# Moving two swaps and a broadcast one step later, and one transpose ahead, in a fused attention kernel

## The chip, the cores and the metric

The kernel runs on one core of a Trainium2 chip. A core has five engines that run their own instruction streams side by side: TensorE (PE; its weight loads are shown as PEld), VectorE (DVE), ScalarE (ACT), GpSimd (POOL) and SyncE (SP), which here does nothing but issue DMAs. DMAs issued by SP and by POOL are carried by the same 16 DMA engines. The metric is the device time of one execution in microseconds (us), the median over runs.

## The reference

Three layers follow one another, all in fp32. Attention with pooled queries comes first; its output is cut into tokens for a dense layer with the Mish activation, and that layer's output goes to eight experts whose gates come from a Sinkhorn iteration.

```python
q_pool = q.reshape(B, H, S // 2, 2, D).mean(axis=3)          # B=2, H=8, S=1152, D=64
scores = scale * np.matmul(q_pool, k.transpose(0, 1, 3, 2))
scores = scores - np.max(scores, axis=-1, keepdims=True)
attn = np.exp(scores)
attn = attn / (np.sum(attn, axis=-1, keepdims=True) + 1e-09)
x = np.matmul(attn, v)                                        # -> tokens (1152, 512)
h = x @ w_in;  x = (h * np.tanh(softplus(h))) @ w_out         # w_in (512, 2048)
P = sinkhorn(exp(x @ w_gate))                                 # 8 rounds, 8 experts
out = sum(P[:, e:e+1] * (np.maximum(x @ w1[e], 0) @ w2[e]) for e in range(8))
```

The change touches the attention alone.

## The kernel before

Every fp32 product is made of parts: a value is split into a rounded high part and a low rest (names ending in h and l), and the high and low parts are multiplied separately into one sum. For the attention, one 128-column weight tile carries high and low of 64 head dimensions side by side, and the second copy with the halves swapped gives the cross products.

The attention works on 8 pairs of heads. A pair has 2 x 576 pooled queries, that is 9 tiles of 128 queries (t = 0 to 8; t = 4, the middle one, belongs half to each head). One loop runs over all 72 tiles; its body, one step (number g, pair p, tile t), works on several tiles at once:

- PE makes the scores of tile g (psS, line 478), DVE evacuates them and takes the row minimum of the negated scores (e, line 483), ACT takes the exponential with its row sum (line 497).
- In step g + 1 SP issues the hand-over of that tile, a DMA from `e` to `er` (line 503) that copies the tile as it is into another buffer. `er` has two buffers: the hand-over of tile g can start only when PE has transposed tile g - 2.
- In step g + 3 PE transposes tile g out of `er` (psT, line 560), ACT and DVE evacuate it in halves (eth, line 563; etl, line 566), and over the steps after that PE multiplies it with V (psA, line 581).

Beside these run the preparations of the next pair, a little in each step. POOL splits K, V and Q and issues their loads (kraw, vraw, qraw). PE transposes the split K in thirds (psk, line 410) and the split Q in three pieces (psq, line 456): the first, u = 0, in step t = 6 of the pair before, the second, u = 1, in step t = 1, the third, u = 2 (the middle tile), in step t = 0. ACT copies each piece out (qT, line 463; qz, line 429). A piece then needs a second copy with its two 64-row halves exchanged: `swap` (line 450), two SBUF-to-SBUF DMAs. The first piece is used from t = 0 of its pair, the middle one at t = 4, the second from t = 5.

The row sums of a pair are finished after its last tile: `turn_sums` (line 510) runs at the end of step t = 1 of the next pair. PE turns the sums, DVE copies them (rt, line 515), SP writes them to DRAM (row, line 520) and reads them back broadcast over the partitions in three DMAs (rx, line 526). POOL multiplies the pair's output with rx at the end of step t = 5 (xs, line 607).

What sets the order: all of it is written out by hand, each engine runs its instructions in program order, and SP is one queue. An SP instruction that waits holds everything behind it. Work for SP that has to wait for a result is put in the list `first` and issued at the start of the next step, ahead of that step's hand-over:

```python
waiting = first + loads
first[:], loads[:] = [], []
for f in waiting:
    f()
...
if pre:
    pre.pop(0)()            # the first transposes of this step, ahead of psT
...
    transposes(g - LAG)     # psT, LAG = 3
if g <= NQ:
    hand_over(g - 1)        # e -> er
```

The other transposes of a step (what is left in `pre`) come after its psA, ahead of its exponential.

Of the kernel before, what the change touches and what calls it, by code (L numbers as in the profile page):

```python
# [23 lines left out]
def pool_attention_mish_sinkhorn_kernel(  # L24
# [22 lines left out]
    NPAIR = B * H // 2  # L47
# [59 lines left out]
    def run(t, eng, most=99):  # L107

        q = queue[eng]
        while q and q[0][0] <= t and most > 0:  # L110
            q.pop(0)[1]()
            most -= 1
# [185 lines left out]
    with ExitStack() as actx:  # L298
        def pool(name, bufs, **kw):
            return actx.enter_context(tc.tile_pool(name=name, bufs=bufs, **kw))  # L300
# [29 lines left out]
        for i in range(2):  # L330
            t = z_p.tile([P, 2, 2, P], F32R, name=f"qz{i}")
# [2 lines left out]

        raws, kst, vst, kT, qst, qT = {}, {}, {}, {}, {}, {}
        loader = nc.sync
        loads, first = [], []

        def heads(p):
            b, hp = divmod(p, HPB)  # L340
# [78 lines left out]
        def q_tile(p, x):  # L419
            u, i = divmod(x, MID)  # L420
            if (p, u) not in qT:
                qT[p, u] = qt_p.tile([P, 2, MID, P], F32R, tag="qT", name=f"qT{p}_{u}", bufs=2)
            return qT[p, u], i

        def middle(p, ps, n):

            z = qz[p % 2]
            for j in range(2):
                nc.scalar.activation(
                    z[:, 0:n, j, j * D:(j + 1) * D], ps[:, 0:n, j * D:(j + 1) * D].bitcast(F32), AF.Copy)  # L430
# [16 lines left out]
        def swap(t):  # L447

            for a, b in ((0, D), (D, 0)):
                nc.sync.dma_start(out=t[a:a + D, 1].bitcast(F32), in_=t[b:b + D, 0].bitcast(F32))  # L450

        def trans_q(p, u):
            ps = ps_t.tile([P, 4, P], F32R, tag="t", name=f"psq{p}_{u}")
            n = min(MID, QTL - MID * u)
            for i in range(n):
                nc.tensor.transpose(  # L456
                    ps[:, i, :], qst[p][:, MID * u + i, 0:2, :].rearrange("p a d -> p (a d)"), identr)
            if u == 2:
                middle(p, ps, 1)
                t = qz[p % 2]  # L460
            else:
                t, _ = q_tile(p, MID * u)
                nc.scalar.activation(t[:, 0], ps[:, 0:n].bitcast(F32), AF.Copy)
            first.append(lambda: swap(t))

        scS, eS, erS, rsS, rxS = {}, {}, {}, {}, {}

# [42 lines left out]
        def turn_sums(p):  # L510

            ps = ps_t.tile([P, 4, P], F32, tag="t", name=f"psr{p}")
            nc.tensor.transpose(ps[0:QTL, 0, :], rsS.pop(p), ident)
            rt = rx_p.tile([QTL, P], F32, tag="rt", name=f"rt{p}")
            nc.vector.tensor_copy(rt, ps[0:QTL, 0, :])
            row = row_p.tile([QTL, P], F32, tag="row", name=f"row{p}")
            rx = rxS[p] = rx_p.tile([P, SQ], F32, tag="rx", name=f"rx{p}")

            def out():
                nc.sync.dma_start(out=row, in_=rt)  # L520
                first.append(back)

            def back():
                flat = row.rearrange("t p -> (t p)")
                for j, x, a, n in ((0, 0, 0, SQ), (1, 0, SQ + D, SQ - D), (1, SQ - D, SQ, D)):
                    nc.sync.dma_start(
                        out=rx[j * D:(j + 1) * D, x:x + n], in_=flat[a:a + n].unsqueeze(0).to_broadcast([D, n]))

            first.append(out)
# [86 lines left out]
        def run_av(n):  # L616
            for _ in range(n):
                if av_todo:
                    av_todo.pop(0)()
# [79 lines left out]
        def turn(p, t):  # L699
            fs = []  # L700
            for j in range(2):
                pp = p + (j == 0)
                if pp < NPAIR:
                    fs += [
                        lambda pp=pp, j=j, c=c: trans_k(pp, j, c)
                        for c in range(3) if TURN["k10" if p == 0 and j == 1 else f"k{j}"][c] == t]
            for u in range(3):
                pp = p + (u == 0)
                if p == 0 and TURN["q0"][u] == t:
                    fs.append(lambda u=u: trans_q0(u + 2))  # L710
                if 0 < pp < NPAIR and TURN["q"][u] == t:
                    fs.append(lambda pp=pp, u=u: trans_q(pp, u))
            return fs

        for g in range(T0 + EARLY):
            p, t = divmod(g, QTL)
            if g == 1:
                bctx.close()
                ps_t = pool("ps_t", 4, space=PSUM)
                ps_a = pool("ps_a", 1, space=PSUM)  # L720
            pre = turn(p, t) if g < NQ else []
            waiting = first + loads
            first[:], loads[:] = [], []
            for f in waiting:
                f()
            if g < LAG:
                exps(g)
                for f in pre:
                    f()
                if g + 1 < LAG:  # L730
                    split_kv(0, 0, "v", nc.gpsimd, g)
                    scores(g + 2, ps_s)
            else:
                if LAG < g < NQ:
                    scores(g)
                if p and g < NQ:
                    prep(p, t)
                if g < T0:
                    run(g, "dve")
                if pre:  # L740
                    pre.pop(0)()
                if t == 7 and 0 < p < NPAIR:
                    run_av(4)
                ready = len(av_todo)
                if g < NQ + LAG:
                    transposes(g - LAG)
                if g <= NQ:
                    hand_over(g - 1)
                if not p:
                    prep(p, t)  # L750
                run_av(min(ready, (5 if t == 6 and 0 < p else 9) if g < NQ else 18))
                for f in pre:
                    f()
                if g < NQ:
                    exps(g)
            if p and t == 0:
                row_sums(p - 1)
            if p and t == 1:
                turn_sums(p - 1)
            if late:  # L760
                late.pop(0)()
            if g < T0:
                run_all(g)
            if g == QTL:
                load_gate()
            if g == NQ - 1:
                sctx.close()
                ps_o = ctx.enter_context(tc.tile_pool(name="ps_o", bufs=3, space=PSUM, side="right"))
                wpools["d0"] = ctx.enter_context(tc.tile_pool(name="wd0", bufs=1, side="right"))
                mctx = ExitStack()  # L770
                wpools["d1"] = mctx.enter_context(tc.tile_pool(name="wd1", bufs=1, side="right"))
                wpools["t"] = mctx.enter_context(tc.tile_pool(name="wt2", bufs=3, side="right"))
            if g >= T0:
                mish_step(g - T0)
# [559 lines left out]
```

## Time and profile before

| What | Value |
|---|---|
| Median of 3 runs | 1222.17 us (1221.45 to 1222.9) |
| The profiled execution | 1223.26 us |
| Its span, first to last instruction | 1221.5 us, granted TensorE clock 1.000 |
| PE busy | 1203.7 us, 99% of the span |
| DVE, POOL, ACT busy | 855.8, 654.0, 592.1 us |
| Chain that ended last | PE 90%, DVE 5%, DMA 4%, ACT 1%, issue 1% |
| Largest DMA group | er<-e, 70 issues of 576.0 KB, 4.1 us to landing (median) |

The chain says on what the end of the program hung, step by step backwards; the engine with the largest share of it is the one whose work or waiting set the time. The attention occupies about the first 262 us, 72 steps of some 3.5 us each; behind it come the dense layer and the experts. In the rows below, a DMA issue is shown on `SPq` with the line that issued it, `x3` says that three were merged into one row, and a bracket such as `[0.93 <-DMA er<-e]` gives the idle time of the engine just before the instruction and what ended it.

### The profile page before, as it was taken

The page shows a single profiled execution, that of the slowest core. Times are in us where ns is not written, and L with a number is a line of the kernel's source. Part 1 is how long each engine was busy: PE and PEld are TensorE (multiplying, and loading weights), DVE is VectorE, ACT ScalarE, POOL GpSimd, SP SyncE. Part 2 cuts the span into 40 slices and gives each one's busy share as a digit, 9 for nine tenths or more (in the row PEclk, how much of TensorE's full clock was granted, in tenths as well). Part 3 has the DMA queues.
Part 4 walks back from the last instruction along what each step waited for, and adds up shares of the span by engine and source line. Part 5 has one row for each costly group of instructions (what it writes and reads, how often), then busy time and mean ns, then how long its engine had stood idle before and what let it go on. Part 6 is the DMA issues. An engine that isn't in the chain of part 4 may idle for free.

```text
span 1221.5 us, 19362 instructions
## 1 busy us (share of the span) xinstructions
PE 1203.7 (99%) x6840; PEld 1110.4 (91%) x6840; DVE 855.8 (70%) x1598; ACT 592.1 (48%) x1354; POOL 654.0 (54%) x752
## 2 busy tenths in 40 slices
PE   8899999999999999999999999999999999999998
PEld 8899999999999999898888889999888889999887
DVE  7899999876444333787866677766866777866865
ACT  7888889877544443543332233333333233333331
POOL 7667777415444331485755566555555565555551
PEclk9999999999999999999999999999999999999999
DMA  6787787653223210011111111111011111111112
GB/s 202 265 281 263 272 264 255 232 179 120 88 71 98 74 31 30 1 52 53 32 38 45 52 48 49 52 52 52 23 40 52 53 44 52 53 52 38 37 39 78
DMA packets 51985, 116.39 MB, mean 95 GB/s; under 512 B 7977, under 2 KB 22897, under 8 KB 51889
## 3 DMA queue, kind: packets, MB, share of 16 engines
q1 hardware_dynamic: 48400, 103.36, 25.9%
q0 software_dynamic: 3488, 11.80, 3.3%
q8 instruction: 54, 0.88, 0.3%
q14 instruction: 43, 0.34, 0.1%
HBM read 66.86 MB, written 2.40 MB: 57 GB/s over the span
## 4 chain that ended last, share of the span: by engine, by line
PE 90%; DVE 5%; DMA 4%; ACT 1%; issue 1%; POOL 0%; POOLq 0%; ACTq 0%
PE po L1237 30%; PE c L1067 26%; PE ph L231 10%; PE po L806 8%; PE psS L478 4%; PE psA L581 4%; DMA er<-e 4%; PE psT L560 3%; DVE e L483 2%; DVE etl L566 1%; PE psk L410 1%; PE psw L646 0%; ACT eth L563 0%; PE pg L861 0%; PE psq L456 0%
## 5 line engine op out<-in xcount | busy, mean ns | idle before, releaser
L83 POOL TENSOR_TENSOR wslotsl<-s,wslotsh 128x256 fp32r<-128x256 f32 x180 | 132.0, 743 | 237.1 <-ACT wslotsh L76 237.1
L1245 DVE SCALAR_TENSOR_TENSOR oacc<-po,Pm,oacc 128x512 f32<-128x512 f32 (+1 forms) x217 | 161.1, 746 | 102.2 <-PE po L1237 95.8
L1237 PE MATMUL po<-wdbl,hhall 128*128 128x512 f32 (+1 forms) x543 | 214.4, 395 | 0.0
L1237 PE MATMUL po<-wdbh,hlall 128*128 128x512 f32 (+1 forms) x543 | 214.1, 394 | 0.0
L1237 PE MATMUL po<-wdbh,hhall 128*128 128x512 f32 (+1 forms) x543 | 214.0, 394 | 0.0
L1084 ACT ACTIVATE t<-c 128x384 f32<-128x384 f32 x80 | 39.3, 491 | 246.2 <-PE c L1067 246.2
L1104 ACT ACTIVATE hhall<-c 128x384 fp32r<-128x384 f32 x180 | 88.6, 492 | 127.4 <-DVE c L1100 124.7
L1237 PEld LDWEIGHTS po<-wdbh,hhall 128*128 128x128 f32 x543 | 102.1, 188 | 24.3
L1237 PEld LDWEIGHTS po<-wdbl,hhall 128*128 128x128 f32 x543 | 102.1, 188 | 23.3
L1237 PEld LDWEIGHTS po<-wdbh,hlall 128*128 128x128 f32 x543 | 102.1, 188 | 23.2
L83 POOL TENSOR_TENSOR wslotsl<-rawu,wslotsh 128x256 fp32r<-128x256 f32 x120 | 90.9, 772 | 49.8 <-ACT wslotsh L76 49.8
L483 DVE TENSOR_SCALAR_CACHE_REDUCE e<-psS 128x1152 f32<-128x1152 f32 x72 | 97.3, 1352 | 22.0 <-PE psS L478 11.7
L566 DVE TENSOR_TENSOR etl<-psT,eth 128x384 fp32r<-128x384 f32 (+1 forms) x240 | 108.0, 507 | 4.8 <-ACT eth L563 4.2
L563 ACT ACTIVATE eth<-psT 128x384 fp32r<-128x384 f32 (+1 forms) x240 | 92.8, 477 | 15.6 <-PE psT L560 15.2
L1105 DVE SCALAR_TENSOR_TENSOR hlall<-c,hhall 128x384 fp32r<-128x384 f32 x180 | 98.7, 548 | 2.1
L1067 PE MATMUL c<-x2l,wslotsh 128*128 128x384 f32 x280 | 94.3, 337 | 0.0
L1067 PE MATMUL c<-x2h,wslotsl 128*128 128x384 f32 x280 | 94.1, 336 | 0.0
L1067 PE MATMUL c<-x2h,wslotsh 128*128 128x384 f32 x280 | 93.8, 335 | 0.0
L497 ACT ACTIVATE e<-e,nm 128x1152 f32<-128x1152 f32 x70 | 89.3, 1276 | 0.1
L175 POOL TENSOR_TENSOR wt<-wt,raw 128x512 int32<-128x512 int32 x32 | 42.4, 1325 | 84.0 <-DVE wt L169 59.8
L478 PE MATMUL psS<-kT,qT 128*128 128x384 f32 x384 | 81.9, 348 | 2.8 <-DVE e L483 2.7
L76 ACT ACTIVATE wslotsh<-s 128x256 fp32r<-128x256 f32 x180 | 72.0, 411 | 24.3 <-DVE s L1033 24.3
(365 smaller groups left out, 3117.2 us busy)
## 6 DMA issues: line engine op xcount, KB each, us to landing
er<-e SPq DMA_DIRECT2D x70, 576.0 KB, 4.1
rawd<-in_moe_w_dram SPq DMA_DIRECT2D x60, 256.0 KB, 2.7
rawu<-in_moe_w_dram SPq DMA_DIRECT2D x30, 384.0 KB, 3.3
raw<-in_moe_w_in_dram SPq DMA_DIRECT2D x16, 512.0 KB, 4.3
raw<-in_moe_w_out_dram SPq DMA_DIRECT2D x16, 512.0 KB, 3.7
vraw<-in_v_dram POOLq DMA_DIRECT2D x15, 288.0 KB, 4.7
kraw<-in_k_dram POOLq DMA_DIRECT2D x13, 288.0 KB, 4.6
qT<-qT SPq DMA_DIRECT2D x28, 128.0 KB, 3.1
```

The costliest lines, as they stand in the source:

```text
L83: eng.tensor_tensor(out=lo, in0=src, in1=hi.bitcast(F32), op=ALU.subtract)
L231: nc.tensor.matmul(ps[:, 0:TH], lhsT=a, rhs=b, start=(n == 0), stop=(n == len(ops) - 1))
L478: nc.tensor.matmul(ps[:, kb, 0:TH], lhsT=a, rhs=kt[:, kb * TH:(kb + 1) * TH], start=(n == 0), stop=(n == len(ops) - 1))
L483: nc.vector.tensor_scalar(sc, ps[:, :, 0:TH], -1.0, None, op0=ALU.mult, op1=ALU.min, accum_out=nm)
L497: nc.scalar.activation(e, sc, AF.Exp, bias=nm, scale=-1.0, accum_out=rsS[p][:, t:t + 1])
L563: nc.scalar.activation(eh[:, cs, o:o + b - a], ps[:, 0:3, a:b], AF.Copy)
L566: nc.vector.tensor_tensor(out=el[:, cs, o:o + b - a], in0=ps[:, 0:3, a:b], in1=eh[:, cs, o:o + b - a].bitcast(F32), op=ALU.subtract)
L806: nc.tensor.matmul(ps[:, 0:TH], lhsT=a, rhs=b, start=(n == 0), stop=(n == len(ops) - 1))
L1067: nc.tensor.matmul(cb[c], lhsT=a_, rhs=b_, start=FIRST[n] and m == 0, stop=LAST[n] and m == len(ops) - 1, skip_group_check=True)
L1105: los.append(lambda: nc.vector.scalar_tensor_tensor(out=lo, in0=b, scalar=0.0, in1=hi.bitcast(F32), op0=ALU.max, op1=ALU.subtract))
L1237: nc.tensor.matmul(ps[:, 0:w], lhsT=a, rhs=b[:, cs], start=(n == 0), stop=(n == len(ops) - 1))
L1245: nc.vector.scalar_tensor_tensor(out=oa, in0=ps[:, 0:w], scalar=gate, in1=oa, op0=ALU.mult, op1=ALU.add)
```

## The change

Three things are moved; nothing is added or taken away.

- The swap of the first piece (u = 0) is issued as before at the start of the next step. The swaps of the second and the middle piece go through the list twice, so they are issued one step later: the middle one at the start of step t = 2 in place of t = 1, the second at t = 3 in place of t = 2.
- The broadcast of the row sums (`back`) also goes through the list twice: at t = 4 in place of t = 3, except for the last pair.
- In step t = 6 the transposes of the first piece are put at the head of the step's transposes. So they run in front of psT, and the third of K that stood there runs after psA.

The unused list `loads` goes away, and with a line less the lines behind it move up by one.

```diff
@@ trans_q
-            first.append(lambda: swap(t))
+            first.append((lambda: swap(t)) if u == 0 else lambda: first.append(lambda: swap(t)))
@@ turn_sums
             def out():
                 nc.sync.dma_start(out=row, in_=rt)
-                first.append(back)
+                first.append(back if p == NPAIR - 1 else lambda: first.append(back))
@@ turn
                 if 0 < pp < NPAIR and TURN["q"][u] == t:
-                    fs.append(lambda pp=pp, u=u: trans_q(pp, u))
+                    fs.insert(0 if u == 0 else len(fs), lambda pp=pp, u=u: trans_q(pp, u))
@@ the loop over the steps
-            waiting = first + loads
-            first[:], loads[:] = [], []
+            waiting, first[:] = list(first), []
```

What SP issues in steps t = 1 to t = 4 of pair 4, before (the rows with L503 are the hand-overs of tiles 0, 1, 2 and 3, one a step):

```order
L450 DMA qz_139<-qz_139 64x256 x2
L503 DMA er_2208<-e_2114 128x1152
L450 DMA qT_1_2186<-qT_1_2186 64x512 x2
L520 DMA row_2225<-rt_2223 9x128
L503 DMA er_2270<-e_2174 128x1152
L526 DMA rx_2226<-row_2225 64x576
L526 DMA rx_2226<-row_2225 64x512
L526 DMA rx_2226<-row_2225 64x64
L503 DMA er_2330<-e_2237 128x1152
L141 DMA raw_0_3_2343<-in_moe_w_in_dram 128x512
L503 DMA er_2384<-e_2296 128x1152
```

And in the changed kernel, the same stretch of SP:

```order
L503 DMA er_2206<-e_2114 128x1152
L450 DMA qz_139<-qz_139 64x256 x2
L520 DMA row_2223<-rt_2221 9x128
L503 DMA er_2268<-e_2172 128x1152
L450 DMA qT_1_2184<-qT_1_2184 64x512 x2
L503 DMA er_2327<-e_2235 128x1152
L141 DMA raw_0_3_2340<-in_moe_w_in_dram 128x512
L526 DMA rx_2224<-row_2223 64x576
L526 DMA rx_2224<-row_2223 64x512
L526 DMA rx_2224<-row_2223 64x64
L503 DMA er_2384<-e_2293 128x1152
```

The middle swap (qz) has moved behind the hand-over of tile 0, the second swap (qT_1) behind that of tile 1, and the broadcasts (rx) behind that of tile 2 and behind the weight load (raw) that follows it. All of them still stand ahead of the hand-over of tile 3.

What ACT does in step t = 6 of pair 4, before (kT is a third of the next pair's K, eth the halves of psT, qT_0 the first piece of the next pair's queries, the last row the exponential):

```order
L411 ACTIVATE kT_0_2414<-psk_0_1_2467 128x384
L563 ACTIVATE eth_1_2420<-psT_0_2472 128x3x128
L563 ACTIVATE eth_1_2420<-psT_1_2478 128x3x128
L563 ACTIVATE eth_1_2420<-psT_2_2484 128x3x128
L463 ACTIVATE qT_0_2502<-psq_0_2497 128x512
L497 ACTIVATE e_2464,rs_2161<-e_2464,nm_2465 128x1152
```

And in the changed kernel:

```order
L463 ACTIVATE qT_0_2472<-psq_0_2467 128x512
L563 ACTIVATE eth_1_2420<-psT_0_2474 128x3x128
L563 ACTIVATE eth_1_2420<-psT_1_2480 128x3x128
L563 ACTIVATE eth_1_2420<-psT_2_2486 128x3x128
L411 ACTIVATE kT_0_2414<-psk_0_1_2499 128x384
L497 ACTIVATE e_2464,rs_2161<-e_2464,nm_2465 128x1152
```

The copies of qT_0 and kT have changed places; the swap of qT_0, which waits for the first, can be issued that much earlier.

## Rows read from the trace of the kernel before

**Rows 1.** Windows: busy us by engine (x instructions), clock, DMA share, GB/s.
```profile
120.00:180.00 60.00, 58.92 (x455) 56.22 (x455) 55.57 (x114) 53.97 (x122) 47.58 (x52) 1.00 0.79 264
```

**Rows 2.** Waits of PE in 8 to 265: total us, times, longest.
```profile
PE psT L560 <- DMA er<-e: 7.6, 8, 2.0
```

**Rows 3.** Timeline of PE: start, duration, instruction, idle before it and releaser.
```profile
36.62 0.25 PE L560 MATMUL psT<-identr,er 128*128 128x128 f32 x1 [1.03 <-DMA er<-e]
...
59.67 0.34 PE L560 MATMUL psT<-identr,er 128*128 128x128 f32 x2 [1.96 <-DMA er<-e]
...
87.99 0.34 PE L560 MATMUL psT<-identr,er 128*128 128x128 f32 x2 [0.41 <-DMA er<-e]
...
116.40 0.34 PE L560 MATMUL psT<-identr,er 128*128 128x128 f32 x2 [0.45 <-DMA er<-e]
...
120.35 0.25 PE L560 MATMUL psT<-identr,er 128*128 128x128 f32 x1 [0.60 <-DMA er<-e]
...
180.65 0.34 PE L560 MATMUL psT<-identr,er 128*128 128x128 f32 x2 [0.93 <-DMA er<-e]
...
216.85 0.33 PE L560 MATMUL psT<-identr,er 128*128 128x128 f32 x2 [1.67 <-DMA er<-e]
```

**Rows 4.** Timeline of SP, pair 5: start and duration of issues.
```profile
167.59 1.11 SPq L450 DMA_DIRECT2D qz<-qz  x2
...
169.54 1.67 SPq L450 DMA_DIRECT2D qT<-qT  x2
...
172.96 0.48 SPq L503 DMA_DIRECT2D er<-e  x1
175.55 1.75 SPq L526 DMA_DIRECT2D rx<-row  x3
177.40 0.53 SPq L503 DMA_DIRECT2D er<-e  x1
...
181.66 0.49 SPq L503 DMA_DIRECT2D er<-e  x1
```

**Rows 5.** The chain in order of time, pair 5: start, us until landed.
```profile
172.96 7.55 DMA er<-e
```

**Rows 6.** Windows as in rows 1: the burst of pair 1, of pair 5, its end.
```profile
46.00:60.00 14.00, 12.04 (x98) 11.80 (x97) 10.19 (x21) 10.69 (x22) 12.72 (x15) 1.00 0.96 324
172.00:184.00 12.00, 11.07 (x84) 10.36 (x83) 10.16 (x22) 8.62 (x18) 5.23 (x8) 1.00 0.96 289
184.00:188.00 4.00, 3.94 (x37) 3.93 (x37) 3.57 (x6) 3.85 (x10) 3.83 (x4) 1.00 0.69 278
```

**Rows 7.** DMA issues by line, attention: times, KB each, median us to landing.
```profile
qT<-qT SPq DMA_DIRECT2D x26, 128.0 KB, 3.0
...
rx<-row SPq DMA_DIRECT2D x7, 144.0 KB, 4.9
rx<-row SPq DMA_DIRECT2D x7, 128.0 KB, 4.6
```

**Rows 8.** Waits of SP, whole program: total us, times, longest.
```profile
SPq L526 <- DMA row<-rt: 11.5, 8, 2.5
```

**Rows 9.** Timeline of SP, pair 6: broadcasts and the hand-over of tile 2.
```profile
208.98 1.75 SPq L526 DMA_DIRECT2D rx<-row  x3
210.83 0.53 SPq L503 DMA_DIRECT2D er<-e  x1
```

**Rows 10.** Timeline of SP, pair 0, steps t = 6 and 7.
```profile
26.85 0.47 SPq L503 DMA_DIRECT2D er<-e  x1
28.98 1.12 SPq L450 DMA_DIRECT2D qT<-qT  x2
```

**Rows 11.** Line 503 in 181.6 to 181.7, tile 3 of pair 5: landing.
```profile
DMA to landing us min/median/max: 5.0/5.0/5.0
```

**Rows 12.** Timeline of PE: psT of tile 3, pair 5.
```profile
187.26 0.93 PE L560 MATMUL psT<-identr,er 128*128 128x128 f32 x9
```

**Rows 13.** Timeline of POOL: the product with rx, pair 4's sums.
```profile
183.93 1.42 POOL L607 TENSOR_TENSOR xs<-xs,rx 128x576 f32<-128x576 f32 x1 [6.07 <-DVE xs L598]
```

More of the change, by code (lines that the diff above doesn't have):

```diff
@@ L336, in pool_attention_mish_sinkhorn_kernel @@
         loader = nc.sync
-        loads, first = [], []
+        first = []
         def heads(p):
```

## The prediction

> **What bounds the kernel now.** I read the page's busy lines and its chain first: PE leads both by far, and behind the attention nothing but PE's own work shows, so a microsecond that PE loses or wins in the attention is lost or won at the end. The windows of the attention came next: in 60 us PE is busy 58.92, DVE 55.57, ACT 53.97, and the DMA engines are busy 79% of the time [rows 1]. PE is nearly full, so what can be won there is what it waits. The list of PE's waits gives one cause worth the name: psT, the transposes of a tile, waited for its hand-over 8 times, 7.6 us in all [rows 2]. The timeline of PE shows where: seven of the eight are in [rows 3]; the eighth, the rest of the total, lies in the start-up. Sorted by tile they are: 1.03 us at tile 6 of pair 0; 1.96 us at tile 3 of pair 1; 0.41 us at tile 2 of pair 2; 0.45 and 0.60 us at tiles 1 and 2 of pair 3; 0.93 us at tile 1 of pair 5; 1.67 us at tile 2 of pair 6. So the waits sit where the swaps, the broadcasts and the loads of the next pair come together.
>
> The timeline of SP shows how. In pair 5 the second swap (issued 169.54) stands ahead of the hand-over of tile 1 (172.96), the three broadcasts (175.55) ahead of that of tile 2 (177.40) [rows 4]. The hand-over of tile 1 needed 7.55 us [rows 5]; in that time the DMA engines were busy 96% at 289 GB/s [rows 6]. Two prices follow. A swap of the second piece is 2 x 128 KB [rows 7], 262,144 bytes, and at 289 GB/s takes 0.91 us of the engines. The broadcasts are 144 + 128 + 16 KB, 294,912 bytes, or 1.02 us. A second cost is SP's own: the broadcasts wait for the row to land in DRAM, 11.5 us over 8 pairs [rows 8], and take 1.75 us to issue, and the hand-over stands behind both. In pair 6 it left at 210.83, when the broadcasts had begun at 208.98 [rows 9].
>
> **The change part by part.**
>
> *Tiles 1 and 2 get a free way.* Ahead of the hand-over of tile 1 there is now the middle swap in place of the second one, issued some 3 us before it, right behind the hand-over of tile 0. So 0.91 us of engine time goes from its front, and the broadcasts no longer run beside its end. The wait of pair 5 was 0.93, that of pair 3 0.45: both go. Ahead of tile 2 stands the second swap (0.91 us of transfer) in place of the broadcasts (1.02 us), and SP neither waits for the row nor spends the 1.75 us. The hand-over of pair 6 can leave up to 210.83 - 208.98 = 1.85 us earlier; its wait was 1.67. So I count the five waits as gone: 0.41 + 0.45 + 0.60 + 0.93 + 1.67 = 4.06 us. The bounds: 4.06 if nothing else takes their place, 0 if POOL's query loads, which start beside the hand-over of tile 1, and not SP's work are what holds it. I take 4.06, since in pairs 5 and 6 the time set free is about as long as the wait.
>
> *The second swap enters the burst.* Before, it was issued at 169.54, ahead of the stretch in which the engines are full; now it goes right behind the hand-over of tile 1, about 173.5. Nothing leaves the queue ahead of tile 3: middle swap, second swap, row, weight load and broadcasts all still precede it. So by the end of the burst the engines have up to 0.91 us more to do. In pair 1 there is no slack: 46 to 60 is busy 96% at 324 GB/s [rows 6], and tile 3 already waited 1.96 us. There I add 262,144 bytes at 324 GB/s, 0.81 us. In pair 5 the hand-over of tile 3 left at 181.66 and took 5.0 us, so it landed at 186.66 [rows 4, 11], and psT came at 187.26 [rows 12]: 0.60 us of slack. The 0.93 us won at tile 1 pull psT forward to 186.33, so 0.33 us short, if the landing stays; and if the landing also slips by 0.91, 1.24 us. But from 184 to 188 the engines are busy only 69% [rows 6], so 1.24 us of those 4 are free to take it up. The bounds for a pair are thus 0 and 1.24 us. I take 0.30 for each of pairs 2 to 5, near the 0.33, because the burst ends with room; 1.20 us in all. For pair 6, which has no query load behind it, I take 0.
>
> The Trainium skill (DMA: Bandwidth & Descriptors, section Queues, rings and completion order) says that each DMA engine takes up the descriptors of one issuing queue in ring order and alternates between queues packet by packet. By it the broadcasts only change the tile that they delay, from 2 to 3, and the change would win nothing; here the trace agrees so far that the hand-over of tile 1 took 7.55 us in the full stretch, against a hand-over of 5.0 us where the stretch ends. What that would cost stands below as a rival.
>
> The same page (section Specifications) gives a ceiling of 435 GB/s for the fabric; by that a swap would take an estimated 0.60 us, and pair 1 would lose 0.60 and not 0.81. The measured 324 GB/s decides.
>
> *The first piece's transposes go ahead.* The same transposes and copies run in the same step, so PE and ACT pay nothing; the third of K that goes behind psA is not used before the next pair. The swap can be issued right behind the hand-over of the step, in pair 0 at about 26.85 + 0.47 = 27.3 in place of 28.98 [rows 10], 1.6 us earlier, and so is out of the way of tile 6, for which PE waited 1.03 us. I take 0.70; bounds 0 (the engines were full anyway) and 1.03. In the other pairs no wait stands behind that swap: 0.
>
> *The broadcasts land later.* POOL needs rx in step t = 5. In pair 5 it began the product at 183.93, after waiting 6.07 us for DVE [rows 13]. The broadcasts would now be issued about 178 and land, with the median of 4.9 us [rows 7], at about 183: just in time, perhaps a microsecond late. POOL has 12 us in 60 free [rows 1] and nothing that PE waits for follows at once. I take 0; if POOL's cover were gone, DVE's next write into the same xs tile would be late next. The two swaps are used at t = 4 and t = 5, two steps after their new place: 0.
>
> **The sum.** -4.06 - 0.70 + 0.81 + 1.20 = -2.75 us. Against the profiled execution, whose 1223.26 us are its span of 1221.5 and 1.8 around it, that makes 1220.5. That execution lies 1.1 above the median of 1222.17; against the median the forecast is 1219.4.
>
> **The rivals.**
>
> *The wait moves whole to tile 3.* The five waits go, but pairs 2 to 5 pay 1.0 us each at tile 3, pair 1 its 0.81, and pair 0 gains nothing: -4.06 + 4.0 + 0.81 = +0.75, or 1222.9. For it: the bytes ahead of tile 3 are the same and the engines were full from 172 to 184. Against it: the 31% free behind.
>
> *Slower: tile 3 is hit by both the swap and the broadcasts.* If the free share at the end of the burst can't be used, because the hand-over of tile 3 sits in SP's queue directly behind broadcasts that themselves go slowly, it lands 0.91 + 1.02 = 1.93 us later. With 0.60 us of slack that is 1.33 us at tile 3 in each of the pairs 1 to 6, 8.0 us, against 4.06 won: +3.9, or 1226.1. It decides from a delay of tile 3 of about 0.6 + 4.06 / 6 = 1.3 us on. For it: raw and rx now stand back to back right in front. Against it: the hand-over of tile 3 is issued last, some 4 us behind them.
>
> *The waits stay.* The loads of POOL's queue, not SP's, fill the engines beside the hand-over of tile 1: the landings come as before, 1222.2. Against it: the 1.85 us at which SP held tile 2 in pair 6 belong to SP alone.
>
> *All is won.* No new wait at tile 3, none in pair 1, and all of pair 0's: -4.06 - 1.03 = -5.1, or 1217.1.
>
> **How the numbers follow.** A measurement of this kernel tells a difference of about 0.2%, 2.4 us, from none. Forecast, with its own range from 1217.1 to 1221 and the all-won case as its lower end: 0.60, of which 0.46 lies beyond 2.4 us and 0.14 within. Wait moved whole: 0.20, within but for 0.02 slower. Waits stay: 0.08, within. Slower: 0.12, of which 0.10 is beyond. Faster 0.46, same 0.42, slower 0.12. The range goes from 1217.0, all won, to 1224.0, half-way from no change to the slower case.
>
> **What would show it.** Right: psT of tiles 1 and 2 without idle time in front in pairs 2 to 6; SP's hand-over of tile 2 right behind psT, with no wait for the row ahead of it; the waits for er at tile 3 of pairs 1 to 5 together under 4.5 us; no wait at tile 6 of pair 0. The steps would be wrong if tile 1 of pairs 3 and 5 still waits, if tile 3 waits more than 1 us in most pairs, or if DVE or PE waits show POOL's xs behind rx.

## The result: slower by 1.3%, and the profile after

| | before | after |
|---|---|---|
| Median, measured side by side | 1221.81 us (1220.49 to 1222.9) | 1237.73 us (1235.98 to 1240.91) |
| Ratio, 95% interval | | 1.0134 [1.0110, 1.0158] |
| Profiled execution; its span | 1223.26; 1221.5 us | 1238.59; 1236.8 us |
| Granted TensorE clock | 1.000 | 0.993 |

The change costs 16 us where 2.8 us of gain were forecast. All of it lies in the attention. These are the last scores of the attention in PE's timeline, first in the kernel before, then in the changed one: they begin 15.2 us later, the whole difference of the spans but 0.1.

```profile
254.87 1.34 PE L478 MATMUL psS<-kT,qT 128*128 128x384 f32 x6 [0.27 <-DVE e L483]
```
```profile
270.10 1.31 PE L478 MATMUL psS<-kT,qT 128*128 128x384 f32 x6 [0.27 <-DVE e L483]
```

The window that answers to [rows 1] has the same columns. PE fell from 58.92 busy us to 56.95, DVE rose from 55.57 to 56.32, GpSimd (POOL) fell from 47.58 to 40.45, the clock from 1.00 to 0.97 and the DMA engines' share from 0.79 to 0.72. So the DMA engines have less to do per microsecond, and VectorE, of all engines, is busier:

```profile
120.00:180.00 60.00, 56.95 (x422) 52.87 (x421) 56.32 (x101) 49.99 (x113) 40.45 (x44) 0.97 0.72 235
```

PE's waits in the attention (total us, times, longest) answer to [rows 2]. The hand-overs, 7.6 us in 8 waits, became 5.1 in 3; waits for DVE, before 2.7 us for `e` and 0.7 us for other things, took their place:

```profile
PE psS L478 <- DVE e L483: 5.6, 8, 1.5
PE psT L560 <- DMA er<-e: 5.1, 3, 2.6
PE psq L456 <- DVE etl L566: 3.3, 3, 1.5
```

In PE's timeline, tile 6 of pair 0 has lost its wait, and the three that are left for a hand-over are all at a tile 3, of the pairs 1, 2 and 4. At tiles 1 and 2, where five of the seven rows of [rows 3] stand, none is left:

```profile
33.86 0.92 PE L560 MATMUL psT<-identr,er 128*128 128x128 f32 x9
...
57.61 0.93 PE L560 MATMUL psT<-identr,er 128*128 128x128 f32 x9 [2.58 <-DMA er<-e]
...
91.93 0.93 PE L560 MATMUL psT<-identr,er 128*128 128x128 f32 x9 [2.03 <-DMA er<-e]
...
165.02 0.93 PE L560 MATMUL psT<-identr,er 128*128 128x128 f32 x9 [0.49 <-DMA er<-e]
```

SP's timeline of pair 5 answers to [rows 4]: hand-over of tile 1, second swap, hand-over of tile 2, weight load, broadcasts, hand-over of tile 3 (first of the three in the last row).

```profile
185.58 0.48 SPq L503 DMA_DIRECT2D er<-e  x1
186.11 1.45 SPq L450 DMA_DIRECT2D qT<-qT  x2
189.62 0.48 SPq L503 DMA_DIRECT2D er<-e  x1
190.15 0.59 SPq L141 DMA_DIRECT2D raw<-in_moe_w_out_dram  x1
190.86 2.45 SPq L526 DMA_DIRECT2D rx<-row  x3
194.22 6.94 SPq L503 DMA_DIRECT2D er<-e  x3
```

The broadcasts are not only issued a step later, they also take longer to land. Their landing times over pairs 2 to 6 (line 526, 78 to 240 us), first before, then after:

```profile
DMA to landing us min/median/max: 3.2/4.9/5.9
```
```profile
DMA to landing us min/median/max: 5.3/6.4/8.9
```

GpSimd's product, which answers to [rows 13], now waits for them and not for DVE, here in pair 5. In the pairs 2 to 6 it stands 9.2 to 10.5 us in front of the product, where it stood 5.1 to 7.3 before, four of five times for rx by the list (the fifth names a DVE instruction). Counted from VectorE's last write into xs, which the product needs too, the product begins 4.2, 2.0, 1.1, 1.8 and 0.5 us late; before it followed within 0.1 us in four of the five pairs and within 0.5 in the fifth:

```profile
198.50 1.44 POOL L607 TENSOR_TENSOR xs<-xs,rx 128x576 f32<-128x576 f32 x1 [10.23 <-DMA rx<-row]
```

Behind the product GpSimd works without a pause to the end of the pair, so it stays late into the next one. There stand two small kinds of VectorE instructions, and these grew. Groups of DVE's instructions by line (busy us, mean ns; 30 us to the end of the attention), before and after:

```profile
L160 DVE SCALAR_TENSOR_TENSOR wt<-raw,mask 128x256 uint32<-128x256 uint32 x12 | 6.2, 517 | 0.0
L507 DVE TENSOR_TENSOR rs<-rs,eps 128x9 f32<-128x9 f32 x8 | 1.6, 206 | 0.0
```
```profile
L160 DVE SCALAR_TENSOR_TENSOR wt<-raw,mask 128x256 uint32<-128x256 uint32 x12 | 16.7, 1390 | 0.0
L507 DVE TENSOR_TENSOR rs<-rs,eps 128x9 f32<-128x9 f32 x8 | 7.2, 904 | 0.0
```

One place shows how. Of pair 4, DVE's timeline (first fence), GpSimd's (second) and PE's (third; kernel after in all). Line 160, 0.42 us in its median before, takes 3.23 here: it begins beside a GpSimd instruction and ends 0.3 us after the last of four, when GpSimd stands for a moment in front of a DMA issue. Line 507 begins beside one GpSimd instruction and ends with the next (143.34 and 143.98). DVE's next evacuations begin that much later, and PE stood 1.54 us for one of them. The chain that ended last tells the same of the whole run: DVE's lines 160 and 507 and the broadcasts' landing hold 1% of it each, and none of the three is in the chain's list of before.

```profile
138.84 3.23 DVE L160 SCALAR_TENSOR_TENSOR wt<-raw,mask 128x256 uint32<-128x256 uint32 x1
141.99 1.47 DVE L566 TENSOR_TENSOR etl<-psT,eth 128x384 fp32r<-128x384 f32 x3
143.39 0.47 DVE L598 TENSOR_TENSOR xs<-psA,avt 64x320 f32<-64x320 f32 x1
143.78 1.66 DVE L507 TENSOR_TENSOR rs<-rs,eps 128x9 f32<-128x9 f32 x1
```
```profile
137.68 1.44 POOL L388 TENSOR_TENSOR qraw<-qraw 128x576 f32<-128x576 f32 x1
139.09 0.68 POOL L80 TENSOR_SCALAR vst<-vraw 128x576 fp32r<-128x576 f32 x1
139.73 0.67 POOL L390 TENSOR_SCALAR qraw<-qraw 128x576 f32<-128x576 f32 x1
140.38 1.40 POOL L83 TENSOR_TENSOR vst<-vraw,vst 128x576 fp32r<-128x576 f32 x1
142.08 0.58 POOL L347 DMA_DIRECT2D vraw<-in_v_dram  x1 [0.30 <-POOL vst L83]
...
143.34 0.68 POOL L80 TENSOR_SCALAR qst<-qraw 128x576 fp32r<-128x576 f32 x1
143.98 1.42 POOL L83 TENSOR_TENSOR kst<-kraw,kst 128x576 fp32r<-128x576 f32 x1
```
```profile
142.59 0.54 PE L456 MATMUL psq<-identr,qst 128*128 128x128 f32 x4 [1.54 <-DVE etl L566]
```

**The sum of the difference.** The waits of PE listed from 8 us to the end of the attention were 11.0 us before and are 16.4 after, 5.4 more. The rest is PE's busy time, 1203.7 before and 1213.5 after, 9.8 more for the same instructions, and most of that is its clock, as the last section shows. 5.4 + 9.8 = 15.2, beside 15.3 of span.

### The profile page after: what moved, and what is told of

Read it like the earlier page. It is cut to its first block, busy times and chain, and to the rows that moved or that the text cites. A ratio compares the mean times of both kernels' runs of the same rounds, so it can differ in the third digit from the quotient of the medians.

```text
span 1236.8 us, 19381 instructions
## 1 busy us (share of the span) xinstructions
PE 1213.5 (98%) x6840; PEld 1115.7 (90%) x6840; DVE 872.6 (71%) x1598; ACT 592.7 (48%) x1354; POOL 653.0 (53%) x752
## 3 DMA queue, kind: packets, MB, share of 16 engines
q1 hardware_dynamic: 48400, 103.36, 26.1%
## 4 chain that ended last, share of the span: by engine, by line
PE 89%; DVE 6%; DMA 2%; issue 1%; ACT 1%; SPq 0%; POOL 0%; DVEq 0%; ACTq 0%; POOLq 0%
PE po L1236 30%; PE c L1066 25%; PE ph L231 10%; PE po L805 8%; PE psS L478 5%; PE psA L581 4%; PE psT L560 3%; DVE etl L566 2%; DMA er<-e 2%; DVE e L483 1%; DVE wt L160 1%; PE psk L410 1%; DVE rs L507 1%; DMA rx<-row 1%; ACT e L497 0%
## 5 line engine op out<-in xcount | busy, mean ns | idle before, releaser
L563 ACT ACTIVATE eth<-psT 128x384 fp32r<-128x384 f32 (+1 forms) x240 | 92.8, 477 | 14.1 <-PE psT L560 13.9
L497 ACT ACTIVATE e<-e,nm 128x1152 f32<-128x1152 f32 x70 | 89.2, 1274 | 10.6 <-issue 8.3
L478 PE MATMUL psS<-kT,qT 128*128 128x384 f32 x384 | 85.0, 358 | 5.7 <-DVE e L483 5.6
L581 PE MATMUL psA<-etl,vst 128*128 128x256 f32 (+1 forms) x288 | 83.1, 311 | 1.2 <-DVE xs L598 0.7
```

What stands on the lines that cost most here:

```text
L478: nc.tensor.matmul(ps[:, kb, 0:TH], lhsT=a, rhs=kt[:, kb * TH:(kb + 1) * TH], start=(n == 0), stop=(n == len(ops) - 1))
L563: nc.scalar.activation(eh[:, cs, o:o + b - a], ps[:, 0:3, a:b], AF.Copy)
L581: nc.tensor.matmul(box["ps"][:, 0:n], lhsT=vst[p, j][:, c].rearrange("p a d -> p (a d)"), rhs=(el, eh)[which][:, c, 0:n], start=(c == 0 an ...
```

## The experiments

Theory A: late broadcasts make GpSimd late, and late GpSimd holds VectorE's instructions up. Theory B, the prediction's slower rival: the late broadcasts lie in front of tile 3's hand-over. Each ratio is to the kernel before, run on the same chip, with its 95% interval.

### Undo the broadcasts' move

```diff
-                first.append(back if p == NPAIR - 1 else lambda: first.append(back))
+                first.append(back)
```
(against the changed kernel)

> The changed kernel with the broadcasts put back to t = 3; the swaps and the first piece's transposes stay moved. Theory POOL (the broadcasts land about 4 us later, POOL stands in front of its product with rx, and all its later work of the pair then falls on DVE's two instructions with two SBUF inputs, the shift of the weights on line 160 and the add of eps on line 507): 1217 to 1222 us, line 160 under 8 us in sum and line 507 under 2 us as before, xs begins within 2.5 us of the step's scores. Theory SWAPS (the later swaps or the exchanged transposes of t = 6 do it): 1233 us or more, lines 160 and 507 still at 16 and 7 us.

Measured: 1.0056 [1.0037, 1.0074], 1227.93 us, between the ranges of the two theories. Taken out of the whole change, the broadcasts' move is 0.8% of the 1.3%. Lines 160 and 507 are back at 7.8 and 1.8 us. But PE waits 8.8 us for hand-overs, and the rest of the change is still a loss.

### The broadcasts' move alone

```diff
-                first.append(back)
+                first.append(back if p == NPAIR - 1 else lambda: first.append(back))
```
(against the kernel before)

> The kernel before with the broadcasts alone moved to t = 4. Theory POOL: 1232 to 1240 us, line 160 about 16 us and line 507 about 7 us in sum, POOL's wait for rx some 9 us in pairs 2 to 6. Theory SWAPS: 1220 to 1224 us.

Measured: 1.0114 [1.0101, 1.0127], 13.9 us; lines 160 and 507 at 14.1 and 5.9 us, waits for hand-overs 6.4 us. This one line of the change makes most of its loss by itself. The broadcasts stand behind the weight load here too, and landed after 3.6 to 8.3 us, 4.8 in the median, as before; so that place by itself does not make the slower landings of the changed kernel.

### The swaps' move alone

```diff
-            first.append(lambda: swap(t))
+            first.append((lambda: swap(t)) if u == 0 else lambda: first.append(lambda: swap(t)))
```

> The kernel before with the swaps of the second and middle queries a step later, the broadcasts at their old place and the first piece behind the exponentials as before. Theory: the run with the broadcasts early and the other two parts in took 1.0056 of before; if the first piece is worth -0.7 us, the swaps alone cost +6 to +8 us in the median, because the second swap now stands in the step of the broadcasts' landing and tile 2 waits about 1.6 us in four pairs (er 8 to 9 us in all), plus what the clock takes. Rival: the swaps alone are worth what the prediction said, -2 us (tiles 1 and 2 gain 4.1, tile 3 loses 2.0), and the scatter of that run came from somewhere else.

Measured: 1.0067 [1.0046, 1.0088], so the theory and not its rival: the swaps alone cost, and gain nothing. SP's timeline of pair 5 shows the reason: the second swap has left the front of tile 1 (173.31), and stands, together with the broadcasts, in front of tile 2 (177.88):

```profile
173.31 0.48 SPq L503 DMA_DIRECT2D er<-e  x1
173.84 1.62 SPq L450 DMA_DIRECT2D qT<-qT  x2
175.56 2.21 SPq L526 DMA_DIRECT2D rx<-row  x3
177.88 0.52 SPq L503 DMA_DIRECT2D er<-e  x1
```
PE's waits in this kernel (8 to 290 us):
```profile
PE psT L560 <- DMA er<-e: 8.4, 9, 1.4
```
It is 0.8 us more than before, in nine places, the four longest (1.43, 1.41, 1.35 and 0.89 us) at tile 2. The profiled execution took 1223.81 us at clock 1.000, 3.9 above the median of the kernel before on this chip; the other five ran to 1232.84 us at clocks of 0.994 to 0.999. So part of the 7.6 us goes with the clock and part is there without it. Taking each execution's lost clock off its time, an estimate from the clocks and spans on record, leaves a median of 1225.3 against 1219.6. Which waits make this part was not settled: the trace of before is one execution of 1223.26 us, itself above this chip's median of 1219.94.

### The first piece alone

```diff
-                    fs.append(lambda pp=pp, u=u: trans_q(pp, u))
+                    fs.insert(0 if u == 0 else len(fs), lambda pp=pp, u=u: trans_q(pp, u))
```

> The kernel before with one edit alone: the first piece of the queries is turned in front of the exponentials of its step; swaps and broadcasts where they were. The stall in front of pair 0's tile 6 (0.53 and 0.70 us) should go and nothing else move: about 0.7 us less than before, span 1219.5 to 1220.5 us beside a before of 1220.2. Rival: the piece ahead of the exponentials keeps PE from nothing but takes ACT's evacuation ahead of them, so scores of the next step wait for e: 1 to 3 us more than before.

Measured: 0.9986 [0.9972, 0.9999], 1.7 us faster, by the interval just so. The waits for hand-overs fell to 3.7 us, more than tile 6 had to give. Pair 1's 1.96 us at tile 3 is gone too, which the edit does not touch, so the places of the waits change from one execution to another; the interval does not tell whether the rest belongs to the edit.

### Late GpSimd, no transfer moved

```diff
+                if p < NPAIR - 1:
+                    for _ in range(3):
+                        nc.gpsimd.tensor_tensor(out=idle, in0=idle, in1=idle, op=ALU.add)
```
(behind the division in `split_x`, against the kernel before)

> The kernel before, no DMA moved; POOL gets three idle 128x576 adds (1.43 us each, 4.3 us) behind each pair's product, for pairs 0 to 6, so that it is as late as in the changed kernel. Theory POOL: lines 160 and 507 grow by 10 us or more together and the time rises by 8 to 16 us, though no transfer has changed place. Rival DMA (the late broadcasts slow the hand-overs, POOL's lateness is harmless because PE waits for nothing of POOL's): less than 2 us.

Measured: 1.0201 [1.0188, 1.0214], 24 us more, above what was expected. Lines 160 and 507 took 26.1 and 8.5 us. Three additions of 1.15 us, on an engine that has 12 us in 60 free [rows 1], cost 3.5 us for each of the seven pairs that have them. The chief waits of PE in it (two lines were added, so L458 here is L456 elsewhere):

```profile
PE psq L458 <- DVE etl L568: 7.9, 4, 2.0
PE psS L480 <- DVE e L485: 5.6, 9, 1.5
PE psk L412 <- POOL kst L83: 4.7, 5, 1.2
```
The third is GpSimd's own: PE waits for its K directly. Theory A's mechanism holds; whether it is the changed kernel's is not shown by this run.

### GpSimd's product a step later

```diff
-                    late.append(lambda: late.append(lambda: split_x(p)) if p < NPAIR - 1 else split_x(p))
+                    late.append(lambda: late.append(lambda: late.append(lambda: split_x(p))) if p < NPAIR - 1 else split_x(p))
```
(against the changed kernel, with a second `xs` buffer)

> The changed kernel with POOL's product also one step later, at the end of t = 6, with a second xs buffer: the broadcasts stay late, but POOL does its work of t = 5 and 6 in front of the wait. Theory POOL: back to 1216 to 1224 us, lines 160 and 507 at most 3 us over before. Rival DMA: 1230 us or more.

Measured: 1.0121 [1.0108, 1.0134]. Lines 160 and 507 are back at 8.2 and 2.7 us, and the time is not. PE's waits for hand-overs doubled, from 5.1 to 10.6 us, up to 3.9 us at one tile 3:

```profile
PE psT L560 <- DMA er<-e: 10.6, 5, 3.9
```
So theory A alone fell here. A reading that fits, and that the next run tests: in the changed kernel VectorE's delay had made PE late enough that tile 3 more often found its hand-over landed.

### The product without the sums, and nothing broadcast

The first of these multiplies xs of pairs 0 to 6 by itself, so that GpSimd does not wait, with every transfer as in the changed kernel; the second does not send the broadcasts of these pairs either.

```diff
-                nc.gpsimd.tensor_tensor(out=xs, in0=xs, in1=rxS.pop(p), op=ALU.mult)
+                nc.gpsimd.tensor_tensor(out=xs, in0=xs, in1=rxS.pop(p) if p == NPAIR - 1 else xs, op=ALU.mult)
```
```diff
-                first.append(back if p == NPAIR - 1 else lambda: first.append(back))
+                if p == NPAIR - 1:
+                    first.append(back)
```

> The changed kernel, except that GpSimd's product of pairs 0 to 6 multiplies xs by itself and not by the broadcast sums (the division by the row sums is left out there); all transfers, the late broadcasts too, are issued as in the changed kernel. Theory A (GpSimd is late because it waits for the broadcasts, and its later instructions hold VectorE's): the product starts with xs, GpSimd is 4 us earlier, lines 160 and 507 are back at 6 to 9 and 1.6 to 2.5 us (after: 16.7 and 7.2), and the time falls to 1223 to 1229 us. Theory B (the late broadcasts lie in front of tile 3's hand-over, and its wait and the clock make the loss): lines 160 and 507 fall too, but PE's waits for er grow to 8 to 11 us as with the product a step later, and the time stays at 1232 to 1238 us.

Measured: 1.0106 [1.0083, 1.0130], 1233.26 us: theory B's figures, the waits even above them. Lines 160 and 507 stand at 6.3 and 1.9 us, and PE waits for hand-overs in six places, five of them the tile 3 of pairs 1 to 5 (3.58, 2.66, 2.73, 1.32, 1.56 us):

```profile
PE psT L560 <- DMA er<-e: 12.1, 6, 3.6
```

SP did not issue these hand-overs later: in the pairs 2 to 5 that of tile 3 left 0.8 us behind the start of its step's score evacuation, as it did in the changed kernel and in the version without both causes below. It landed 8.2, 8.4, 6.8 and 7.1 us after its issue, against 5.0, 5.1, 4.8 and 5.1 us in that version. So the time goes in the transfer, not in SP's queue in front of it.

> As the run before in this list, and the broadcasts of pairs 0 to 6 are not sent at all (the division is left out there, the last pair keeps both). Neither cause is left. Both theories: nothing in front of tile 3 but the second swap, GpSimd on time: 1217 to 1221 us, PE's waits for er under 3 us in all. If it stays above 1226 us, the two other edits (swaps, first piece) cost by themselves what neither theory has.

Measured: 0.9964 [0.9949, 0.9979], 1214.65 us, below what was expected. No wait for a hand-over is left; this is the longest of all of PE's waits:

```profile
PE psS L478 <- DVE e L483: 2.7, 4, 1.5
```
The swaps and the first piece cost nothing once the broadcasts are gone: their loss needs the broadcasts beside them.

### Late GpSimd without broadcasts

The three additions of above on the last kernel.

> The run without broadcasts (e8: product of pairs 0 to 6 without the sums, nothing sent, 1214.65 us) with three idle GpSimd additions of 128x576 behind each pair's division (3 x 1.15 us), so that GpSimd is about 3.5 us late as in the changed kernel (there 4.3 us), and no transfer added. With e8 (neither cause), e7 (late broadcasts without GpSimd's wait, 1233.3 us) and the changed kernel (both, 1237.7 us) it makes a table of two by two. Theory (GpSimd late is a cause that suffices by itself): lines 160 and 507 at 14 to 26 and 5 to 8 us, PE's waits for er under 1 us, 1228 to 1238 us. Rival (late GpSimd costs only beside the crowd of transfers; without it the slack takes the stretched instructions up): lines 160 and 507 as high, and 1215 to 1220 us.

Measured: 1.0189 [1.0172, 1.0206], 1244.84 us: late GpSimd without theory B, above the range that theory A gave. No wait for a hand-over appears. Not all of it is VectorE's: PE waits for GpSimd's K directly, 3.4 us in five places, a wait that the changed kernel's list does not have. Line 160 took up to 4.72 us at one time:

```profile
L160 DVE SCALAR_TENSOR_TENSOR wt<-raw,mask 128x256 uint32<-128x256 uint32 x12 | 29.3, 2443 | 0.0
```

With the changed kernel that makes a table of two by two, in us:

| | broadcasts out of the way | broadcasts in front of tile 3 |
|---|---|---|
| GpSimd on time | 1214.65 | 1233.26 |
| GpSimd late | 1244.84 | 1237.73 (the changed kernel) |

Either cause suffices for a loss, and they don't add up; as I read the traces, a PE that is late for one no longer waits for the other. The lower left is late by 3.5 us behind seven products, the lower right only in pairs 2 to 6, and through a wait, so the two of the lower row are not equal in dose: line 160 takes 29.3 us in the one and 16.7 in the other. What theory A would cost at the changed kernel's dose without the broadcasts was not run. In the right column it adds nothing that is clear of the noise: 1.0106 [1.0083, 1.0130] without it, 1.0134 [1.0110, 1.0158] with it.

### One input in place of two

```diff
-            nc.vector.tensor_tensor(out=rs, in0=rs, in1=eps.to_broadcast([P, QTL]), op=ALU.add)
+            nc.vector.tensor_scalar(rs, rs, EPS, None, op0=ALU.add)
```
(against the changed kernel; line 160 likewise becomes the `tensor_scalar` that stands in the other branch of `shift`, now line 164)

> The changed kernel with the two stretched kinds of VectorE instructions rewritten to have one tensor input and immediate numbers: line 160's shift and mask of the weights, and line 507's addition of eps to the row sums. Theory: GpSimd's instructions hold those of VectorE that read two inputs in SBUF; with one input they keep their 0.42 and 0.15 us beside GpSimd (sums 5 to 7 and about 1.2 us, after 16.7 and 7.2), PE's steps 1 to 3 of pairs 3 to 6 fall back to 3.6, 3.8 and 3.25 us, and the waits go back to tile 3, as in the run without the product's wait: 1230 to 1236 us. Rival: any VectorE instruction from SBUF to SBUF is held, whatever its inputs: the sums stay at 14 to 18 and 5 to 8 us and the time at 1236 to 1240 us.

Measured: 1.0154 [1.0124, 1.0185]: the rival's time. The rewritten instructions are still stretched, though the first kind's sum, 12.9 us, lies between the two ranges. So it isn't the number of inputs alone.

```profile
L164 DVE TENSOR_SCALAR wt<-raw 128x256 uint32<-128x256 uint32 x12 | 12.9, 1072 | 0.0
L507 DVE TENSOR_SCALAR rs<-rs 128x9 f32<-128x9 f32 x8 | 6.2, 770 | 0.0
```

Nor is it every instruction from SBUF to SBUF. In the kernel without broadcasts the reciprocal of line 508, which has one input, ran four times beside a GpSimd instruction that had begun before it, and kept its 0.21 to 0.22 us. One of these places, DVE's row and GpSimd's:

```profile
99.82 0.21 DVE L508 RECIPROCAL rs<-rs 128x9 f32<-128x9 f32 x1
```
```profile
99.74 1.44 POOL L83 TENSOR_TENSOR kst<-kraw,kst 128x576 fp32r<-128x576 f32 x1
```

### A version without both causes

The broadcasts of pairs 0 to 6 go out in step t = 8, and GpSimd's product in step t = 3 of the next pair, where GpSimd stood idle (that of pair 6 right behind the attention). Everything is computed. The core of the edit to the changed kernel:

```diff
-                first.append(back if p == NPAIR - 1 else lambda: first.append(back))
+                if p < NPAIR - 1:
+                    backs[p] = back
+                else:
+                    first.append(back)
...
+            if t == 8 and p - 1 in backs:
+                backs.pop(p - 1)()
...
-                    late.append(lambda: late.append(lambda: split_x(p)) if p < NPAIR - 1 else split_x(p))
+                    if p < NPAIR - 1:
+                        prods[p] = lambda: split_x(p)
+                    else:
+                        late.append(lambda: split_x(p))
...
+            if t == (0 if p == NPAIR else 3) and p - 2 in prods:
+                prods.pop(p - 2)()
...
-        xs_p = pool("xs", 1)
+        xs_p = pool("xs", 2)
```

> A version that takes both causes away and computes everything: the changed kernel, with the broadcasts of pairs 0 to 6 sent in step 8 of the pair, where tiles have 6.5 us from issue to need, and GpSimd's product of these pairs in step 3 of the next pair, in GpSimd's idle stretch (a second xs buffer). Theory (the broadcasts' place was the only cost, all waits of tiles go without them): 1215 to 1219 us, PE's waits for er under 2 us, lines 160 and 507 at 6 to 8 and 1.5 to 2.3 us. Rival: wherever 272 KB of broadcast go, some tile's hand-over pays 1 to 2 us a pair, or GpSimd's product in front of the next pair's work makes it late again: 1222 to 1235 us.

Measured: 0.9965 [0.9947, 0.9982], 1215.66 us: faster than before by 4.2 us and than the changed kernel by some 20, and by its ratio equal to the kernel that sends no broadcasts. Lines 160 and 507 took 5.0 and 1.4 us. The second run is the same edit on the kernel before, with swaps and first piece in their old places.

> The same move of broadcasts and product on the kernel before, swaps and first piece where they were. If the swaps held tiles 1 and 2 up by themselves, as the prediction said, half of the waits stay: about 4 us more than the run before in this list, 1219 to 1223 us. If the broadcasts beside the swaps made those waits, the swaps' place is worth nothing once the broadcasts are gone: within 1.5 us of the run before in this list.

Measured: 0.9972 [0.9956, 0.9988], the first within the error: the swaps' place is worth nothing once the broadcasts are gone. PE's waits for hand-overs in the new version (2.2 us, where under 2 were expected), and in the one with the old swaps (L563 here is L560 elsewhere):

```profile
PE psT L563 <- DMA er<-e: 2.2, 4, 0.6
```
```profile
PE psT L563 <- DMA er<-e: 1.4, 2, 0.9
```

## Why the prediction was wrong

**The step that failed: "The broadcasts land later", priced at 0.** Alone it cost 13.9 us, nearly the whole loss. It was asked there whether rx would be in time and whether GpSimd had slack, and both answers were off. The landing was taken at its old median of 4.9 us, and it was 5.3 to 8.9, so the product began up to 4.2 us behind VectorE's last write, in four of the five pairs more than the microsecond allowed for. And "POOL has 12 us in 60 free" is a mean: its long idle time lies in front of the product, and from there it works through to the end of the pair. What follows was overlooked altogether. "Nothing that PE waits for follows at once" looked for releases, and found none; a late GpSimd harms by running beside VectorE's lines 160 and 507, which no wait of VectorE in the profile shows, only the length of these instructions. The trace of before had the sign: its line 160 took 0.42 us in the median, but 0.72, 0.98 and 0.79 in three places, each beside a GpSimd instruction, and line 507 0.15 and once 0.59. This is one of two ways to the loss: with GpSimd on time the late broadcasts still cost 1.0106, by tile 3's hand-over (third point).

These rows are what the Trainium skill's page SBUF — State Buffer, section Who interferes with whom, describes: a VectorE instruction with two inputs in SBUF contends with a GpSimd instruction that reads there, and a `tensor_scalar` can enter a two-port mode that does too. The trace agrees: of the instructions beside GpSimd, line 507 went from 0.15 to 1.66 us, and as a `tensor_scalar` to 1.80, while line 566, with one input in PSUM, stayed at 505 ns in its mean. With GpSimd's lateness seen, it would have spoken against the change.

**Tiles 1 and 2 get a free way: right in the trace, wrong in its cause.** No wait is left there, as forecast. But the 4.06 us were put down to the swaps, and these alone gained nothing (1.0067): the second swap went from tile 1 to tile 2. With the broadcasts gone the old place of the swaps is as good as the new, within the error. So the waits needed the broadcasts beside the swaps.

**The second swap enters the burst: mis-sized.** For tile 3 of pair 1, 0.81 us more was forecast and 2.58 - 1.96 = 0.62 came. For pairs 2 to 5, 1.20 us in all was forecast and 2.03 + 0.49 = 2.52 came; the five pairs' 5.10 us are above the 4.5 that were named as the sign of being right. But this is tile 3 with PE held up by VectorE. With GpSimd on time tile 3 waited 11.85 us in the pairs 1 to 5, 9.9 more than the 1.96 of before. The slower rival, tile 3 hit by swap and broadcasts, had that mechanism right and with 8.0 us nearly its size. It was given 0.12: the DMA engines' 31% free share at the burst's end was taken for room that the hand-over could use, and against the rival stood that the hand-over is issued some 4 us behind the broadcasts.

**The first piece goes ahead: right.** Tile 6 of pair 0 has no wait, and the edit alone is worth 1.7 us [0.1, 3.4] where 0.70 was counted; the interval holds the 0.70 and does not fix the size.

**What it did not count:** that some waits of 1.4 to 2.6 us are paid again in PE's clock, 8.5 us of the changed kernel's time (below). The sum took each microsecond of waiting for one of time.

## What to carry to other kernels

To move a transfer later by a step, follow it to the engine that consumes it, and that engine to every instruction that it will now run beside, not only to those that wait for it: an instruction's length in the profile can change with its neighbour. Read an engine's slack at the place where the delay enters, since a mean over a pair says nothing of it. And when several transfers contend for one burst, shuffling their order passes the wait on to the next tile; here taking the broadcasts out of the burst, to where their consumer also had its idle time, brought a gain of 4.2 us that the new order did not.

## What the runs showed of the hardware

**PE's clock after a wait.** These are windows of one microsecond at tile 3 of pair 2 in the changed kernel (us; busy us of PE, PEld, DVE, ACT, POOL; clock, DMA share, GB/s). PE stood for 2.03 us until 91.93, and in the second microsecond after it began to work again the granted clock went from full, 2.4 GHz, to half, 1.2 GHz, where it stayed for some three microseconds. In these PE is busy all the time, and does five matmuls to a window in place of some ten.

```profile
91.00:92.00 1.00, 0.07 (x1) 0.10 (x2) 0.06 (x1) 0.00 (x0) 1.00 (x1) 1.00 0.57 217
92.00:93.00 1.00, 1.00 (x11) 1.00 (x12) 1.00 (x1) 0.61 (x2) 0.91 (x2) 1.00 0.10 41
93.00:94.00 1.00, 1.00 (x9) 1.00 (x8) 1.00 (x4) 0.64 (x2) 0.92 (x2) 0.57 0.00 0
94.00:95.00 1.00, 1.00 (x5) 1.00 (x5) 0.70 (x2) 0.91 (x2) 1.00 (x2) 0.50 0.97 401
95.00:96.00 1.00, 1.00 (x5) 0.90 (x4) 0.00 (x0) 0.82 (x2) 0.91 (x2) 0.50 1.00 279
96.00:97.00 1.00, 1.00 (x10) 1.00 (x8) 0.86 (x1) 0.49 (x1) 1.00 (x2) 0.72 0.56 172
```

That is 0.43 + 0.50 + 0.50 + 0.28 = 1.71 us of lost clock for one wait. Between 40 and 240 us the changed kernel's windows of 10 us lie below full clock six times (0.95, 0.88, 0.83, 0.83, 0.80, 0.86), 8.5 us in all, the larger part of the 9.8 us by which PE's busy time grew. They belong to four falls, which came behind waits of PE of 2.58, 2.03, 1.54 and 1.42 us (the third in the fence of pair 4 above). The kernel before, with waits of 1.96 and 1.67 us [rows 3], kept 1.00 in all twenty. So the length of the wait alone does not tell whether the clock falls; what decides it was not found.

**How long VectorE can be held.** Line 160 did not wait for one GpSimd instruction but, at its longest, for four in a row: 3.23 us in the changed kernel, and up to 4.83 with the three additions on the kernel before, until GpSimd paused in front of a DMA issue. A pause is not always needed: line 507's 0.43 us in the kernel without broadcasts (99.35) ended with GpSimd's line 80 while line 83 followed at once. What lets VectorE in was not tried by itself.
